# A fused FNet and GEGLU kernel: the first stage in another order

## The chip, the cores and the metric

The kernel runs on one core of a Trainium2 chip. The metric is the device time of one execution in microseconds (us). The engines are named as in the profile: PE is TensorE, PEld its weight loads, DVE is VectorE, ACT is ScalarE, POOL is GpSimd, and SP is SyncE, whose queue issues every DMA.

## What is computed

```python
# x: 2048 rows of 448, fp32; _A_ref is a two-sided DFT (hidden, then sequence; real part)
xn = _layernorm(x)
s = _A_ref(xn, dft_seq_re, dft_seq_im, dft_hid_re, dft_hid_im)
g = silu((gelu(xn @ w_gate) * (xn @ w_up)) @ w_down)      # w_gate, w_up: 448 x 1792
out = x + s * g
```

Every matrix product keeps fp32 accuracy by splitting operands: a rounded part ("high", written by ACT or DVE as fp32r) and the rest ("low", the source minus the high part, written by DVE). A product then is three matmuls: high by high, high by low, low by high.

## The kernel before, in words

The 2048 rows are four chunks (0 to 3) of 512 rows; a chunk is four tiles of 128 rows. The 1792 columns of the feed-forward part are seven groups of two blocks of 128. The order of instructions is written out by hand: the whole body stands under `tc.manual_schedule()`, so each engine executes its own instructions in the order in which the source issues them, and waits at an instruction until what that instruction reads is there. DMAs are issued by SP in the same way, in source order.

The change concerns the first stage, the first 80 us or so, which handles the first group (`GROUPS[0]`) for all four chunks. The steps in it:

- `load_x(c, k0, k1)` (L87) loads tiles of chunk c into `xr`; `load_w(f)` (L167) loads the gate and up weights of one block into one of two `raw` buffers, `load_d` (L219) the down weights of a group, in turn into the same two buffers.
- `stats(c, k0, n)` returns four steps for the layernorm of n tiles. `one(i)` is a BATCH_NORM_STATS (L95) and a BATCH_NORM_AGGREGATE (L96) on DVE for one tile. `root()` is one ACT square root over all n tiles (L100) and two small DVE operations (L101, L102), and so waits for every `one`. `newton()` is four small DVE operations (L106 to L110), the first of which needs the square root. `norm(i)` normalises one tile in place, on DVE (L118) or, if asked, on ACT (L115, L116).
- `turn_mm(c, k)` transposes a normalised tile on PE into a PSUM tile `pt` (L127), of which there are two buffers. `turn_split` empties it: the high part by ACT (L132), a plain copy for later by ACT (L133), the low part by DVE (L134). The third transpose of a chunk can only start when the first `pt` has been emptied by all three.
- `prep_w` splits the weights: high by DVE (L179) or ACT (L177), low by DVE (L182, L184). `prep_d` does so for the down weights (L227 on ACT, L228 on DVE or, for the first group before, on POOL).
- `first` (L417) and `gu_mm` (L239) are the gate and up matmuls. Chunks 0 and 1 are done in halves of 256 columns, `half[0]` from tiles 0 and 1, `half[1]` from tiles 2 and 3 of the chunk.
- `act` starts with a gelu on ACT (L261) and returns three steps, named m, h and l in the source: the product of gelu and up (DVE, L264), its high part (ACT, L265) and its low part (DVE, L266).
- `down` and `down_one` (L286) multiply by the down weights. In the first group ACT copies the results into the accumulator (L293).
- `combine(p)` forms four differences on DVE (L143 to L146) for a Strassen scheme used from the second group on, and returns the step that splits them (L82 on ACT, L83 on DVE).

After the first stage six more groups run through `strassen` (L306, L314 and L286), then the DFT along the hidden axis (L683) and the one along the sequence (L756 to L758).

Of the kernel before, what the change touches and what calls it, by code (L numbers as in the profile page):

```python
# [26 lines left out]
GROUPS = [(f, f + 1) for f in range(0, NF, 2)]  # L27
# [3 lines left out]
def fnet_geglu(ctx: ExitStack, tc: tile.TileContext, x, ct, et, wgu, wd, out):  # L31
# [13 lines left out]
    nc = tc.nc  # L45
# [40 lines left out]
    def load_x(c, k0, k1):  # L86
        nc.sync.dma_start(xr[c][:, k0:k1], xv[:, 4 * c + k0 : 4 * c + k1])  # L87

    def stats(c, k0, n):
        st = const.tile([P, 4, 6], F32, name=f"st{c}_{k0}", tag="st", bufs=2)  # L90
        mv = const.tile([P, 4, 2], F32, name=f"mv{c}_{k0}", tag="mv", bufs=3)
        sd = const.tile([P, 4, 4], F32, name=f"sd{c}_{k0}", tag="sd", bufs=3)

        def one(i):
            nc.vector.bn_stats(st[:, i], xr[c][:, k0 + i, :D])  # L95
            nc.vector.bn_aggr(mv[:, i], st[:, i])  # L96

        def root():
            r, t, w = sd[:, :n, 0], sd[:, :n, 1], sd[:, :n, 2]
            nc.scalar.activation(t, mv[:, :n, 1], AF.Sqrt, bias=epst)  # L100
            nc.vector.tensor_scalar(w, mv[:, :n, 1], EPS, -0.5, op0=ALU.add, op1=ALU.mult)  # L101
            nc.vector.tensor_scalar_mul(sd[:, :n, 3], mv[:, :n, 0], -1.0)  # L102

        def newton():
            r, t, w = sd[:, :n, 0], sd[:, :n, 1], sd[:, :n, 2]
            nc.vector.reciprocal(r, t)  # L106

            nc.vector.tensor_mul(t, r, r)
            nc.vector.tensor_mul(t, t, w)
            nc.vector.scalar_tensor_tensor(r, t, 1.5, r, op0=ALU.add, op1=ALU.mult)  # L110

        def norm(i, eng=nc.vector):
            v = xr[c][:, k0 + i]
            if eng is nc.scalar:
                eng.activation(v, v, AF.Identity, bias=sd[:, i, 3:4])  # L115
                eng.activation(v, v, AF.Copy, scale=sd[:, i, 0:1])  # L116
            else:
                eng.tensor_scalar(  # L118
                    v, v, mv[:, i, 0:1], sd[:, i, 0:1], op0=ALU.subtract, op1=ALU.mult
                )  # L120

        return one, root, newton, norm
# [7 lines left out]
    def turn_split(c, k, pt):  # L130
        sl = slice(k * P, (k + 1) * P)
        nc.scalar.activation(xth[c][:, :, sl], pt, AF.Copy)  # L132
        nc.scalar.activation(xf[c][:, :, sl], pt[:, :2], AF.Copy)  # L133
        nc.vector.tensor_sub(xtl[c][:, :, sl], pt, xth[c][:, :, sl])  # L134
# [26 lines left out]
    def raw_tile():  # L161
        loads[0] += 1
        return a_r[:, 1536 * (loads[0] % 2) :][:, :1536]

    def load_w(f):
        raw = raw_tile()
        nc.sync.dma_start(raw[:, :1024], wgu[f].rearrange("p b f -> p (b f)"))  # L167
        return raw

    def prep_w(slot, raw):  # L170

        w = a_w[:, 2560 * slot : 2560 * slot + 1792]
        wh, wl = w[:, :1024], w[:, 1024:]

        def high(copy):
            if copy is None:
                nc.scalar.activation(wh, raw[:, :1024], AF.Copy)  # L177
            else:
                copy(wh, raw[:, :1024])  # L179

        def low():
            nc.vector.tensor_sub(wl, raw[:, 256:1024], wh[:, 256:])  # L182

            nc.vector.tensor_sub(wh[64:, :256], raw[64:, :256], wh[64:, :256])  # L184

        return high, low, (wh, wl)
# [37 lines left out]
    def prep_d(grp, rv, sub=None):  # L224
        o = 1792 * (grp[0] // 2 % 2)
        w = a_d[:, o : o + 1792].rearrange("p (a f d) -> p a f d", a=2, f=2)
        nc.scalar.activation(w[:, 0], rv, AF.Copy)  # L227
        (sub or nc.vector.tensor_sub)(w[:, 1], rv, w[:, 0])  # L228
        return w

    def gu_mm(ps, w, g, c, cols, late_xtl=False):
        hs, ls = zip(*[block(w, k, g) for k in range(4)])
        hh = [(hs[k], xth[c], k) for k in range(3)]
        hl = [(hs[k], xtl[c], k) for k in range(3)]
        lh = [(ls[k], xth[c], k) for k in range(3)]
        last = [(hs[3], xth[c], 3), (hs[3], xtl[c], 3)]
        mm = hh + lh + last[:1] + hl + last[1:] if late_xtl else hh + hl + lh + last
        for n, (a, xt, k) in enumerate(mm):
            nc.tensor.matmul(ps[:, cols], a, xt[:, k, cols], start=n == 0, stop=n == len(mm) - 1)  # L239
# [8 lines left out]
    def hs_tile(name, dt=FR):  # L248
        return sb.tile([P, 2, 512], dt, name=name, tag="hs", bufs=6)
# [7 lines left out]
    def act(f, c, pg):  # L257
        acts[0] += 1
        gt = tmp(acts[0] % 2)
        hs = new_hs(f, c)  # L260
        nc.scalar.activation(gt, pg[0], AF.Gelu_apprx_tanh)  # L261

        return (
            lambda: nc.vector.tensor_mul(gt, gt, pg[1]),  # L264
            lambda: nc.scalar.activation(hs[:, 0], gt, AF.Copy),  # L265
            lambda: nc.vector.tensor_sub(hs[:, 1], gt, hs[:, 0]),  # L266
        )
# [109 lines left out]
    with tc.manual_schedule():  # L377
        load_x(0, 0, 1)
        load_x(0, 1, 2)
        load_x(0, 2, 4)  # L380
        w_raw = [load_w(0), load_w(1)]
        load_x(1, 0, 4)
        load_x(2, 0, 4)
        load_x(3, 0, 4)
# [39 lines left out]
        one, root, newton, norm = stats(0, 0, 2)  # L424
# [10 lines left out]
        xl = [xtl[0][:, :, k * P : (k + 1) * P] for k in range(4)]  # L435
        nc.scalar.activation(xh[0], t0[2], AF.Copy)
        nc.scalar.activation(xh[1], t1[2], AF.Copy)
        one, root, newton, norm = stats(0, 2, 2)
        one(0)
        one(1)  # L440
        ws = [prep_w(i, w_raw[i]) for i in range(2)]
        ws[0][0](nc.vector.tensor_copy)
        nc.vector.tensor_sub(xl[0], t0[2], xh[0])
        nc.vector.tensor_sub(xl[1], t1[2], xh[1])
        root()
        ws[1][0](None)
        for k, t in enumerate((t0, t1)):
            nc.scalar.activation(xf[0][:, :, k * P : (k + 1) * P], t[2][:, :2], AF.Copy)
        ws[0][1]()
        newton()  # L450
        norm(0)
        norm(1)
# [1 line left out]
        ws = [w[2] for w in ws]  # L454
        draw = load_d(GROUPS[0])
# [4 lines left out]
        one, root, newton, norm = stats(1, 0, 4)  # L460
# [1 line left out]
        one(1)  # L462
        turn_split(*t2)
        turn_split(*t3)
        wdn = prep_d(GROUPS[0], draw, nc.gpsimd.tensor_sub)
        one(2)
        one(3)
        root()
# [8 lines left out]
        turn_split(*t0)  # L477
        turn_split(*t1)
        one, root, newton, norm = stats(2, 0, 4)
        one(0)  # L480
        one(1)
        s_raw = load_w(GROUPS[1][0])
        pg = gu_ps(0, 1)
        gu_mm(pg[0], ws[0], 0, 1, half[0], True)
# [1 line left out]
        gu_mm(pg[1], ws[0], 1, 1, half[0])  # L486
        turn_split(*t2)
        turn_split(*t3)
        m0, h0, l0 = act(0, 0, pgs[0])
        m1, h1, l1 = act(1, 0, pgs[1])  # L490
        m0()
        h0()
        l0()
        gu_mm(pg[0], ws[0], 0, 1, half[1], True)
        gu_mm(pg[1], ws[0], 1, 1, half[1])
        m1()
        h1()
        m0, h0, l0 = act(0, 1, pg)
        one(2)
        l1()  # L500
        one(3)
        root()
        m0()
        h0()
        newton()
        for i in range(4):
            norm(i)
        l0()
        pg = gu_ps(1, 1)
        for g in range(2):  # L510
# [1 line left out]
        one, root, newton, norm = stats(3, 0, 4)  # L512
        one(0)
        one(1)
        xf[2] = hs_tile("xf2", F32)
        turn_split(*turn_mm(2, 0))
        down(0, 0, wdn, [lambda k=k: turn_split(*turn_mm(2, k)) for k in (1, 2, 3)])
        m1, h1, l1 = act(1, 1, pg)
        one(2)
        m1()  # L520
        h1()
        one(3)
        l1()
        root()
        newton()
        norm(0)
        norm(1)

        nws = [None, None]
# [2 lines left out]
        for c in (2, 3):  # L532
            if c == 2:
                draw = load_d(GROUPS[1])
            else:
                s_raw2 = load_w(GROUPS[1][1])
            m0, h0, l0 = gateup(0, c, ws[0])
            between, between1 = [lambda: (m0(), h0()), l0], []
            if c == 2:
                xf[3] = hs_tile("xf3", F32)  # L540
                turn = lambda k: turn_split(*turn_mm(3, k))
                between = [
                    lambda: (m0(), h0(), norm(2)),
                    lambda: (l0(), norm(3), turn(0)),
                    lambda: turn(1),
                    lambda: turn(2),
                ]
                between1 = [lambda: turn(3)]
            down(0, c - 1, wdn, between)
            if c == 2:  # L550
                nws[0] = prep_s(2, s_raw, nc.vector)
            else:
                one = combine(0)
                for i in range(4):
                    one(i)
                nwdn = prep_d(GROUPS[1], draw)
                late_split = combine(1)
            m1, h1, l1 = gateup(1, c, ws[1], between1)
            m1()
            if c == 2:  # L560
                h1()
                l1()
        late = (h1, l1)


# [11 lines left out]
        for gi in range(1, len(GROUPS)):  # L577
            grp = GROUPS[gi]
            nxt = GROUPS[gi + 1] if gi + 1 < len(GROUPS) else None
            ws, wdn = nws, nwdn  # L580
# [226 lines left out]
```

## Time and profile before

| what | value |
|---|---|
| time, median of 3 runs | 813.9 us (813.36 to 814.09) |
| time of the profiled execution | 814.51 us |
| its span, first to last instruction | 812.7 us |
| PE busy | 801.8 us (99%) |
| DVE busy | 415.0 us (51%) |
| ACT busy | 238.7 us (29%) |
| POOL busy | 54.4 us (7%) |
| chain that ended last, PE's share | 95% |
| mean granted PE clock | 0.997 |

The profiled execution is 0.6 us longer than the median, and 1.8 us of its time lie outside its span. Busy shares are averages over the whole span: PE leaves only some 11 us of it idle, so what a change in the order of work is worth has to be read in the windows where PE stands still, by what it waits for there. Times in the trace are counted from the first instruction of the span. A timeline row gives start, duration, engine, line, operation, output and inputs, and in brackets the idle time before it with its releaser.

### The profile page before, as it was taken

What the parts mean: (1) busy time and instruction counts of PE and PEld (TensorE: products, weight loads), DVE (VectorE), ACT (ScalarE), POOL (GpSimd) and SP (SyncE); (2) the same over time, 40 slices, a digit from 0 to 9 for tenths busy, and PEclk for the clock granted to TensorE, in tenths of its full rate; (3) what the DMA queues carried; (4) which work ended last, traced back from release to release, by engine and by line L of the source; (5) the groups of instructions that cost most, each with busy time, mean ns of one, the idle gap of its engine ahead of it and who ended that gap; (6) DMA issues with size and microseconds to landing.
All of it is one profiled execution on the core that took longest, in us unless ns stands there. A gap on an engine that the chain in (4) does not pass through costs nothing.

```text
span 812.7 us, 9386 instructions
## 1 busy us (share of the span) xinstructions
PE 801.8 (99%) x3868; PEld 715.0 (88%) x3868; DVE 415.0 (51%) x626; ACT 238.7 (29%) x356; POOL 54.4 (7%) x62
## 2 busy tenths in 40 slices
PE   8899999999999999999999999999999999999997
PEld 7788888888888888888889999999999999999997
DVE  8776786766776676776763233232232222223221
ACT  3574432322322232232221224122222222222220
POOL 0000120010010010000000000111111111111110
PEclk9999999999999999999999999999999999999999
DMA  8001010000010110100020012344444333444441
GB/s 307 24 0 52 24 52 23 27 27 23 27 49 1 33 43 1 49 23 24 23 77 1 1 38 77 103 140 133 132 127 126 127 127 127 126 127 127 127 127 60
DMA packets 19372, 58.09 MB, mean 71 GB/s; under 512 B 2048, under 2 KB 8064, under 8 KB 18944
## 3 DMA queue, kind: packets, MB, share of 16 engines
q1 hardware_dynamic: 19328, 57.48, 22.1%
q8 instruction: 30, 0.49, 0.2%
q14 instruction: 14, 0.11, 0.0%
HBM read 53.81 MB, written 3.67 MB: 71 GB/s over the span
## 4 chain that ended last, share of the span: by engine, by line
PE 95%; DVE 3%; ACT 1%; issue 1%; DMA 0%; DVEq 0%
PE x L306 22%; PE po L286 16%; PE py L758 13%; PE py L757 13%; PE py L756 13%; PE ab L683 9%; PE x L314 5%; PE gu L239 2%; PE gu L417 1%; PE pt L127 1%; DVE st L95 1%; DVE xr L118 0%; DVE tmp L264 0%; DMA xr<-x 0%; DVE tl L83 0%
## 5 line engine op out<-in xcount | busy, mean ns | idle before, releaser
L286 PE MATMUL po<-wd,hs 128*128 128x448 f32 x672 | 153.0, 366 | 0.0
L286 PEld LDWEIGHTS po<-wd,hs 128*128 128x128 f32 x672 | 125.8, 188 | 14.6 <-ACT gacc L293 0.2
L306 PE MATMUL x<-xt,w 128*128 128x512 f32 x504 | 135.0, 391 | 0.0
L306 PEld LDWEIGHTS x<-xt,w 128*128 128x128 f32 x504 | 94.6, 188 | 17.0
L758 PE MATMUL py<-xt,w 128*128 128x448 f32 x256 | 93.5, 365 | 0.0
L756 PE MATMUL py<-xt,w 128*128 128x448 f32 x256 | 93.5, 365 | 0.0
L757 PE MATMUL py<-xt,w 128*128 128x448 f32 x256 | 93.5, 365 | 0.0
L295 DVE TENSOR_TENSOR gacc<-gacc,po 128x448 f32<-128x448 f32 x96 | 59.3, 618 | 60.8 <-PE po L286 60.8
L306 PE MATMUL x<-th,w 128*128 128x512 f32 x192 | 71.4, 392 | 1.0 <-DVE tmp L264 1.0
L756 PE MATMUL py<-ab,c 128*128 128x448 f32 x192 | 70.1, 365 | 0.0
L757 PE MATMUL py<-ab,c 128*128 128x448 f32 x192 | 70.1, 365 | 0.0
L758 PE MATMUL py<-ab,c 128*128 128x448 f32 x192 | 70.1, 365 | 0.0
L683 PE MATMUL ab<-w,xt 128*128 128x448 f32 x256 | 68.0, 365 | 0.0
L83 DVE TENSOR_TENSOR w<-raw,w 128x1024 fp32r<-128x1024 f32 (+1 forms) x23 | 27.8, 1210 | 73.1 <-ACT w L82 73.1
L82 ACT ACTIVATE w<-raw 128x1024 fp32r<-128x1024 f32 (+1 forms) x23 | 24.2, 1050 | 128.4 <-DMA raw<-ct 118.2
L763 POOL TENSOR_TENSOR gacc<-gacc,s 128x448 f32<-128x448 f32 x15 | 31.0, 2067 | 429.3 <-DVE gacc L762 429.3
L314 PE MATMUL x<-xt,w 128*128 128x512 f32 x192 | 59.2, 389 | 0.0
L762 DVE TENSOR_TENSOR gacc<-gacc,py 128x448 f32<-128x448 f32 (+1 forms) x17 | 10.1, 593 | 87.5 <-PE py L758 87.5
L683 PEld LDWEIGHTS ab<-w,xt 128*128 128x128 f32 x256 | 48.1, 188 | 3.8
L756 PEld LDWEIGHTS py<-xt,w 128*128 128x128 f32 x256 | 48.1, 188 | 3.8
L757 PEld LDWEIGHTS py<-xt,w 128*128 128x128 f32 x256 | 48.1, 188 | 3.8
L758 PEld LDWEIGHTS py<-xt,w 128*128 128x128 f32 x256 | 48.1, 188 | 3.8
(142 smaller groups left out, 1091.1 us busy)
## 6 DMA issues: line engine op xcount, KB each, us to landing
raw<-ct SPq DMA_DIRECT2D x43, 512.0 KB, 4.8
s<-ct SPq DMA_DIRECT2D x21, 512.0 KB, 4.8
raw<-wgu SPq DMA_DIRECT2D x14, 512.0 KB, 3.5
s<-x SPq DMA_DIRECT2D x16, 224.0 KB, 5.2
out<-gacc SPq DMA_DIRECT2D x15, 224.0 KB, 2.0
raw<-wd SPq DMA_DIRECT2D x7, 448.0 KB, 3.3
xr<-x SPq DMA_DIRECT2D x3, 1024.0 KB, 10.9
raw<-et SPq DMA_DIRECT2D x4, 448.0 KB, 3.3
```

The costliest lines, as they stand in the source:

```text
L82: nc.scalar.activation(h, src, AF.Copy)
L83: nc.vector.tensor_sub(l, src, h)
L239: nc.tensor.matmul(ps[:, cols], a, xt[:, k, cols], start=n == 0, stop=n == len(mm) - 1)
L286: nc.tensor.matmul(po[:, :D], hs[:, a, kk * P : (kk + 1) * P], wdn[:, b, i], start=n == 0, stop=n == 5,)
L295: nc.vector.tensor_add(ga, ga, po[:, :D])
L306: nc.tensor.matmul(ps, a[i], b[j], start=first and n == 0, stop=n == 2, skip_group_check=True)
L314: nc.tensor.matmul(ps, w["k3" + "gu"[g]][0], xt[:, 3], start=False, stop=True, skip_group_check=True)
L683: nc.tensor.matmul(p[:, :D], a, b, start=n == 0, stop=n == len(mm) - 1)
L756: nc.tensor.matmul(py[:, :D], a, h, start=k + r == 0, stop=False)
L757: nc.tensor.matmul(py[:, :D], a, l, start=False, stop=False)
L758: nc.tensor.matmul(py[:, :D], b, h, start=False, stop=q == 3 and i == 7)
L763: (nc.vector if last else nc.gpsimd).tensor_add(ga[:, e], ga[:, e], xres[:, e])
```

## The change

It reorders the first stage; no arithmetic is added or left out.

- SP issues the first gate and up weights (`load_w(0)`) as its third DMA, ahead of tiles 2 and 3 of chunk 0, which become the fourth.
- For tiles 2 and 3 of chunk 0, the second `one` and `root` come after the splitting of the first weights instead of before it.
- The low part of the first down weights is formed by DVE instead of POOL, and later: after the l steps of chunk 0, where it had been issued between the second and the third `one` of chunk 1.
- Chunk 2: all four `one` and `root` come before the emptying of chunk 1's third and fourth transposes, where there had been two `one`; `newton` comes before the first gelu, two `norm` between the m, h and l steps of chunk 0, two after `prep_d`. The m and h steps of both blocks now come before their l steps.
- Chunk 3: all four `one` and `root` come before chunk 2's transposes are emptied, where there had been two `one`.
- `combine(0)` is issued after chunk 2 instead of within chunk 3; its splitting stays where it was.
- The order of PE's instructions stays as it was.

```diff
         load_x(0, 0, 1)
         load_x(0, 1, 2)
+        w_raw = [load_w(0)]
         load_x(0, 2, 4)
-        w_raw = [load_w(0), load_w(1)]
+        w_raw.append(load_w(1))
...
+        ws = [prep_w(i, w_raw[i]) for i in range(2)]
+        ws[0][0](nc.vector.tensor_copy)
         one, root, newton, norm = stats(0, 2, 2)
         one(0)
-        one(1)
-        ws = [prep_w(i, w_raw[i]) for i in range(2)]
-        ws[0][0](nc.vector.tensor_copy)
         nc.vector.tensor_sub(xl[0], t0[2], xh[0])
         nc.vector.tensor_sub(xl[1], t1[2], xh[1])
+        ws[1][0](None)
+        ws[0][1]()
+        one(1)
         root()
-        ws[1][0](None)
         for k, t in enumerate((t0, t1)):
             nc.scalar.activation(xf[0][:, :, k * P : (k + 1) * P], t[2][:, :2], AF.Copy)
-        ws[0][1]()
         newton()
...
         turn_split(*t3)
-        wdn = prep_d(GROUPS[0], draw, nc.gpsimd.tensor_sub)
         one(2)
...
         one, root, newton, norm = stats(2, 0, 4)
-        one(0)
-        one(1)
+        for i in range(4):
+            one(i)
+        root()
         s_raw = load_w(GROUPS[1][0])
...
         turn_split(*t2)
         turn_split(*t3)
+        newton()
         m0, h0, l0 = act(0, 0, pgs[0])
         m1, h1, l1 = act(1, 0, pgs[1])
         m0()
         h0()
+        m1()
+        h1()
+        norm(0)
+        norm(1)
         l0()
+        l1()
         gu_mm(pg[0], ws[0], 0, 1, half[1], True)
         gu_mm(pg[1], ws[0], 1, 1, half[1])
-        m1()
-        h1()
+        wdn = prep_d(GROUPS[0], draw)
+        norm(2)
+        norm(3)
         m0, h0, l0 = act(0, 1, pg)
-        one(2)
-        l1()
-        one(3)
-        root()
         m0()
         h0()
-        newton()
-        for i in range(4):
-            norm(i)
         l0()
...
         one, root, newton, norm = stats(3, 0, 4)
         one(0)
         one(1)
+        one(2)
+        one(3)
+        root()
         xf[2] = hs_tile("xf2", F32)
         turn_split(*turn_mm(2, 0))
         down(0, 0, wdn, [lambda k=k: turn_split(*turn_mm(2, k)) for k in (1, 2, 3)])
         m1, h1, l1 = act(1, 1, pg)
-        one(2)
+        newton()
         m1()
         h1()
-        one(3)
+        norm(0)
         l1()
-        root()
-        newton()
-        norm(0)
         norm(1)
...
-                one = combine(0)
                 for i in range(4):
-                    one(i)
+                    late_split(i)
                 nwdn = prep_d(GROUPS[1], draw)
...
             if c == 2:
                 h1()
                 l1()
+                late_split = combine(0)
```

## The prediction

> **What bounds the kernel now.** I read the page first, then the windows of the first 90 us, then the timeline of what ends PE's waits there. The page says that PE is the bound, and that the chain spends only some 5% elsewhere:
>
> ```profile
> PE 801.8 (99%) x3868; PEld 715.0 (88%) x3868; DVE 415.0 (51%) x626; ACT 238.7 (29%) x356; POOL 54.4 (7%) x62
> ...
> PE 95%; DVE 3%; ACT 1%; issue 1%; DMA 0%; DVEq 0%
> ```
>
> So this change is worth what it does to PE's idle time, and to PE's clock. After 18 us PE stands still for 2.10 us at 20.69, 1.15 at 37.88, 0.49 at 42.53 and 1.01 at 80.49. Windows of 1 us, PE alone (busy, then granted clock):
>
> ```profile
> core 0: us, PE busy (x), PEclk, DMA share, GB/s
> 20.00:21.00 1.00, 0.69 (x6) 1.00 0.00 0
> 21.00:22.00 1.00, 0.00 (x0) 1.00 0.00 0
> 22.00:23.00 1.00, 0.21 (x2) 1.00 0.40 77
> 23.00:24.00 1.00, 1.00 (x8) 0.57 0.93 355
> 24.00:25.00 1.00, 1.00 (x6) 0.50 0.07 27
> ...
> 26.00:27.00 1.00, 1.00 (x8) 0.72 0.00 0
> ...
> 37.00:38.00 1.00, 0.88 (x4) 1.00 0.00 0
> 38.00:39.00 1.00, 0.00 (x0) 1.00 0.00 0
> 39.00:40.00 1.00, 0.97 (x7) 1.00 0.00 0
> ```
>
> The wait of 2.10 us is followed by about 3.4 us at half clock (0.57, 0.50, 0.50, 0.72); that of 1.15 us is not. The timeline names the cause of the first and what it costs:
>
> ```profile
> 19.21 2.11 POOL L228 TENSOR_TENSOR wd<-raw,wd 128x896 fp32r<-128x896 f32 x1 [17.91 <-ACT wd L227]
> 19.25 2.10 DVE L101 TENSOR_SCALAR sd<-mv 128x4 f32<-128x4 f32 x1
> ...
> 22.14 1.46 DVE L118 TENSOR_SCALAR xr<-xr,mv,sd 128x512 f32<-128x512 f32 x3
> 22.79 1.61 PE L127 MATMUL pt<-ident,xr 128*128 128x128 f32 x8 [2.10 <-issue]
> 24.05 2.48 PE L417 MATMUL gu<-xt,w 128*128 128x256 f32 x10
> ```
>
> L101 takes 0.17 us elsewhere; beside POOL's subtraction it takes 2.10 and ends with it. The slow clock costs 1.6: eight transposes 1.61 instead of 0.87 (at 14.29), ten L417 matmuls 2.13 in the chain instead of 10 x 0.125. The third and later waits end on DVE:
>
> ```profile
> 40.21 0.69 DVE L266 TENSOR_TENSOR hs<-tmp,hs 128x512 fp32r<-128x512 f32 x1
> 40.81 0.62 DVE L95 BATCH_NORM_STATS2 st<-xr 128x6 f32<-128x448 f32 x1
> ...
> 42.29 1.27 DVE L134 TENSOR_TENSOR xt<-pt,xt 128x512 fp32r<-128x512 f32 x2
> 43.02 0.66 PE L127 MATMUL pt<-ident,xr 128*128 128x128 f32 x4 [0.49 <-DVE xt L134]
> ```
>
> Chunk 2's third transpose waits for L134, which stands behind two `one`. **This is the point to follow**: from 43.02 on PE's work is the same in both kernels and DVE has less left to do, so by how much this transpose comes later or earlier, the end does too.
>
> **Part 1, loads and first weights.** Two DMA answers give the landings:
>
> ```profile
> xr<-x SPq DMA_DIRECT2D x1, 512.0 KB, 4.4
> raw<-wgu SPq DMA_DIRECT2D x1, 512.0 KB, 6.1
> ```
>
> The third DMA (issued 1.63) lands at 6.0, the fourth (2.10) at 8.2. Both are 512 KB, so I let them trade landings: weights at 6.0, rows at 8.2. DVE is free at 6.99 after two L118, as before. L179 takes 0.58 start to start: 7.57. The first `one` now waits for the rows until 8.2 (0.63 lost; none if they land by 7.5, the other bound). Steps from there, start to start: `one` 0.76, two subtractions 0.60 each, L182 0.99, L184 0.45, which gives 11.60. The second `one` ends its aggregate 0.84 later, 12.44; L106 follows 0.37 after that because the square root is no longer hidden behind L182; newton 0.80, two L118 0.92, L182 0.98, L184 0.45: chunk 1's statistics start at 15.96 instead of 14.97, **0.99 late**. PE starts earlier (9.28 becomes about 8.9) but is held by DVE again at the transposes.
>
> **Part 2, POOL's subtraction gone.** L101 comes at 20.24, takes 0.17, and L106 follows at 20.57, 0.33 after L101 started as at 4.95 to 5.28. Three L118 start at 21.37 instead of 22.14, the first transposes at 21.93 instead of 22.79, and at full clock. The second L134 starts at 24.20 (transposes 22.39 to 22.83, ACT's L132, L133, L132, L133 at 0.49 and 0.26 apart from 22.56): chunk 2's statistics start at 24.80 instead of 25.95, **1.15 early**. So removing 2.10 of stall and 1.6 of slow clock leaves 1.15 here.
>
> **Part 3, four `one` and the root of chunk 2 ahead.** Four instead of two: 3 x 0.76 + 0.84 = 3.1, aggregate at 27.93. The wait that this adds is L100's on ACT, and behind it in ACT's queue stand L132 and L133 of chunk 1's last two transposes, for which `half[1]` on PE waits. Before, L132 started at 28.39 by PE's own pace; now at 28.2 by the root, with the second done at 29.55. PE, now faster, is there at 27.70: **a new stall of about 1.85 us**. PE's `half[1]` starts at 29.57 instead of 29.91. The gelu, 2.95 after the first L132 as before (the table load of 1.28 in it), comes at 31.15 instead of 31.34, the first L264 at 31.77.
>
> **Part 4, DVE from there to 43.02.** Start to start: L264 twice 1.2, `norm` twice 0.92, L266 twice 1.2, L228 now on DVE 1.0 (1.08 at 76.98), `norm` twice 0.92, which is 37.0; L264 0.69, ACT's L265 0.63, L266 0.61: 38.98. Four `one` of chunk 3: 42.1. L100 is again ahead of L132 on ACT, so L132 comes at 42.35, L133 at 42.84, L134 at 43.24, and PE's third transpose at **43.95 instead of 43.02: 0.93 late**. PE reaches it at about 40.65 (22 matmuls of 256 columns 2.75, 22 of 512 5.03, two transposes 0.88, twelve L286 2.42): **a new stall of about 3.3 us** in place of 1.15 + 0.49.
>
> **Part 5, edits at nothing.** Two ACT table loads fewer (1.28 each) fall where ACT waits for DVE or PE. The second L219 leaves SP when L228 is done, some 15 us later, and lands well ahead of its L227 at 76.0; behind it in SP's queue is only the L167 that waits until 63.23 in any case. The third L167 moves by 1 us, and its first reader is L200 at 59.60. `combine(0)` goes into DVE's wait of 2.89 before 68.68; yet its split still waits for ACT's L82 at 73.91, behind the last L293, so PE's 1.01 at 80.49 stays. Were the split not held there, the move could gain PE up to that 1.01; were DVE not idle before 68.68, the four subtractions would cost up to 2.8.
>
> **Part 6, the clock, and the sum.** A stall of 2.10 was followed by the slow clock, one of 1.15 was not; 3.3 is beyond both, so I charge 1.6 after it. The stall of 1.85 lies between them, nearer to 2.10. If it too slows PE, that costs nothing itself, since the 3.3 absorbs 1.6 of it. Span: 812.7 + 0.93 + 1.6 = 815.2; with the 1.8 outside, 817.0; the median stands 0.6 below the profiled execution: **816.4 us**.
>
> [...]
>
> **Rivals.** [...] *Rows 2 and 3 land in time*: 0.63 less on the forecast, 815.8. Against: the fourth place landed at 8.2. *The freed stall is kept* (clearly faster): if ACT took L132 ahead of the root, both new stalls would go and 2.10 + 1.6 come off, 810.2; against it stands ACT's strict order in every row here. *Both stalls cost 1.6 in full*: 818.0, only if DVE's chain slips along with PE.
>
> **How the numbers follow.** Forecast 0.50, rows in time with the drop 0.10, both stalls 0.05: slower 0.65. No slow clock 0.31, the same: this kernel's measurement tells about 0.2% (1.6 us) from no change, and 0.93 is less. Faster 0.04. The range runs from 814.2 (no slow clock, rows in time) to 817.6 (the slow clock 1.7, and 1 us for the twenty-odd durations of the chain); the forecast alone is 815.6 to 817.4.
>
> **What would show it.** Right: L101 at about 20.2 with 0.17; L95 of tiles 2 and 3 waiting for a DMA until 8.2; PE idle before `half[1]` near 28 to 29.5, released by ACT L132; PE idle from 40.7 to 43.9, released by DVE L134; clock 0.50 for 3.4 us after it. Wrong: a third transpose of chunk 2 well before 43, or full clock through 50 us.

## The result, and the profile after

The changed kernel takes 816.9 us (median of 8 executions, 816.33 to 818.05), the kernel before, measured beside it, 814.0 (median of 8, 812.90 to 815.95). The ratio is 1.0035 [1.0023, 1.0048]: slower by some 2.9 us. The prediction was 816.4, with a range from 814.2 to 817.6. The profiled execution of the changed kernel took 816.81, its span is 815.0, 2.3 longer than before's 812.7. Two executions of the experiments, of 1740 and 1619 us, lie far outside all others and are left out of every median below.

First the page. PE's work is the same (802.0 busy, x3868); POOL has one instruction less, DVE one more, ACT two less. In the chain, DVE's and a DMA's shares have grown by a point each:

```profile
span 815.0 us, 9383 instructions
...
PE 802.0 (98%) x3868; PEld 714.7 (88%) x3868; DVE 414.6 (51%) x627; ACT 235.7 (29%) x354; POOL 52.0 (6%) x61
...
PE 94%; DVE 4%; ACT 1%; DMA 1%; issue 0%; SPq 0%; DVEq 0%
```

The waits of PE between 12 and 100 us (line that waited, releaser, us in total, times, longest) give the list of places in which to look. The wait of 2.1 at 20.7 is gone; the two longest are new:

```profile
PE pt L127 <- DVE xt L134: 2.9, 1, 2.9
PE gu L239 <- ACT xt L132: 1.6, 1, 1.6
PE x L306 <- DVE tmp L264: 1.0, 1, 1.0
```

The timeline of the changed kernel at those places (start, duration, engine, line, operation; in brackets the idle time before it and what ended it):

```profile
8.62 0.63 DVE L95 BATCH_NORM_STATS2 st<-xr 128x6 f32<-128x448 f32 x1 [0.61 <-DMA xr<-x]
...
16.35 0.63 DVE L95 BATCH_NORM_STATS2 st<-xr 128x6 f32<-128x448 f32 x1
...
20.63 0.17 DVE L101 TENSOR_SCALAR sd<-mv 128x4 f32<-128x4 f32 x1
...
22.43 1.13 PE L127 MATMUL pt<-ident,xr 128*128 128x128 f32 x8 [0.36 <-issue]
...
28.43 0.30 ACT L100 ACTIVATE sd<-mv,epst 128x4 f32<-128x4 f32 x1 [3.69 <-DVE mv L96]
28.63 0.58 ACT L132 ACTIVATE xt<-pt 128x512 fp32r<-128x512 f32 x1
...
30.02 8.07 PE L239 MATMUL gu<-xt,w 128*128 128x256 f32 x44 [1.58 <-ACT xt L132]
...
42.46 0.30 ACT L100 ACTIVATE sd<-mv,epst 128x4 f32<-128x4 f32 x1 [2.39 <-DVE mv L96]
42.67 0.58 ACT L132 ACTIVATE xt<-pt 128x512 fp32r<-128x512 f32 x1
...
43.55 0.69 DVE L134 TENSOR_TENSOR xt<-pt,xt 128x512 fp32r<-128x512 f32 x1 [0.84 <-ACT xf L133]
44.29 1.12 PE L127 MATMUL pt<-ident,xr 128*128 128x128 f32 x4 [2.87 <-DVE xt L134]
```

Read it in pairs. Twice ACT stands idle (3.69 and 2.39) until DVE's aggregate lets L100 go, and only then comes the L132 that stands behind L100 in ACT's queue; twice PE waits for what follows that L132. Without POOL beside it L101 takes 0.17. The windows of PE alone (start and end, length, PE busy and count, granted clock, DMA share, GB/s) show what the second stall brings with it:

```profile
41.00:42.00 1.00, 0.43 (x3) 1.00 0.00 0
42.00:43.00 1.00, 0.00 (x0) 1.00 0.00 0
43.00:44.00 1.00, 0.00 (x0) 0.84 0.00 0
44.00:45.00 1.00, 0.71 (x4) 0.50 0.00 0
45.00:46.00 1.00, 1.00 (x5) 0.50 0.00 0
46.00:47.00 1.00, 1.00 (x4) 0.50 0.00 0
47.00:48.00 1.00, 1.00 (x8) 0.95 0.00 0
```

The clock is at half from 43.68 to 47.10, of which 0.61 still lies in the stall. Further on the chain has the same groups in both kernels (start, duration, engine, output and line). Before:

```profile
44.88 0.44 PE pt L127 x4
...
54.45 1.49 PE po L286 x6
...
61.04 7.53 PE gu L239 x33
```

and in the changed kernel:

```profile
47.46 0.44 PE pt L127 x4
...
57.07 1.23 PE po L286 x6
...
63.36 7.54 PE gu L239 x33
```

The last of them is 2.32 later, which is the difference of the spans. So all of the loss arises ahead of it, in three terms: the third transpose of chunk 2 starts 1.27 later (44.29 for 43.02); from it to the fourth (44.88 and 47.46) PE takes 3.17 for 1.86, 1.31 more, at half clock; and six L286 that took 1.49 before, at 54.45, take 1.23. 1.27 + 1.31 - 0.26 = 2.32.

The first term has to be split once more, as executions do not all get their data at the same time. Chunk 1's statistics begin at 16.35 for 14.97, 1.38 later:

```profile
14.97 0.63 DVE L95 BATCH_NORM_STATS2 st<-xr 128x6 f32<-128x448 f32 x1
```

Counted from there, the third transpose comes after 28.05 before and after 27.94 here. So in this pair of profiles all of the 1.27 is there ahead of chunk 1's statistics; behind them the freed stall and the two new ones cancel, but for 0.11. The experiments say what each of them is worth.

### The profile page after: what moved, and what is told of

Read it like the earlier page. It is cut to its first block, busy times and chain, and to the rows that moved or that the text cites. A ratio compares the mean times of both kernels' runs of the same rounds, so it can differ in the third digit from the quotient of the medians.

```text
span 815.0 us, 9383 instructions
## 1 busy us (share of the span) xinstructions
PE 802.0 (98%) x3868; PEld 714.7 (88%) x3868; DVE 414.6 (51%) x627; ACT 235.7 (29%) x354; POOL 52.0 (6%) x61
## 4 chain that ended last, share of the span: by engine, by line
PE 94%; DVE 4%; ACT 1%; DMA 1%; issue 0%; SPq 0%; DVEq 0%
PE x L306 22%; PE po L286 16%; PE py L759 13%; PE py L757 13%; PE py L758 13%; PE ab L684 9%; PE x L314 5%; PE gu L239 2%; DVE st L95 1%; DMA xr<-x 1%; PE pt L127 0%; PE gu L418 0%; DVE xr L118 0%; DVE tmp L264 0%; ACT xt L132 0%
## 5 line engine op out<-in xcount | busy, mean ns | idle before, releaser
L286 PE MATMUL po<-wd,hs 128*128 128x448 f32 x672 | 153.9, 367 | 0.0
L286 PEld LDWEIGHTS po<-wd,hs 128*128 128x128 f32 x672 | 126.6, 189 | 14.4
```

The lines of the kernel that those rows point to most:

```text
L286: nc.tensor.matmul(po[:, :D], hs[:, a, kk * P : (kk + 1) * P], wdn[:, b, i], start=n == 0, stop=n == 5,)
```

## The experiments

Theory: the loss comes from two orders in ACT's and DVE's queues, the root of chunk 2 ahead of L132 and all of chunk 3's statistics ahead of the emptying, with the slow clock as the second stall's price; what the freed POOL wins is taken back by the first of them. Rivals: the loads and the first weights lose the time; the clock costs nothing; DVE's subtraction is the gain by itself.

Each kernel ran with the kernel before on the same chip; ratios are to that one. First, the changed kernel with one thing altered each time.

**Chunk 3's statistics back where they were, all else changed.**

```diff
         one(1)
-        one(2)
-        one(3)
-        root()
...
         m1, h1, l1 = act(1, 1, pg)
-        newton()
+        one(2)
         m1()
         h1()
-        norm(0)
+        one(3)
         l1()
+        root()
+        newton()
+        norm(0)
         norm(1)
```

> Only chunk 3's statistics go back to their old place: two one ahead of chunk 2's emptied transposes, the other two, root and newton behind. My theory: L134 comes 1.5 (two one) and some 1.1 (the wait for the root on ACT) earlier, the third transpose finds at most 0.3 us of stall, the clock does not fall: 2.6 + 1.3 less, time 812.4 to 813.2, span about 811, under the kernel before. Rival, the late rows of the new load order are the loss: the stage stays late by its 0.6 to 1.0, 816 or more. Rival, the down weights' subtraction on DVE is the loss: it still stands on DVE's chain, 816 or more.

Measured: 813.6 (812.56 to 814.89, 11 executions), ratio 0.9993 [0.9984, 1.0002]; the span is 811.5. The timeline:

```profile
39.16 0.58 ACT L132 ACTIVATE xt<-pt 128x512 fp32r<-128x512 f32 x1
...
41.38 1.27 DVE L134 TENSOR_TENSOR xt<-pt,xt 128x512 fp32r<-128x512 f32 x2
...
42.10 0.66 PE L127 MATMUL pt<-ident,xr 128*128 128x128 f32 x4 [0.20 <-DVE xt L134]
```

L132 comes at 39.16 for 42.67, the wait of 2.87 shrinks to 0.20, and the clock stays at 1.00 behind it. This execution reached chunk 1's statistics at 16.84; counted from there the third transpose comes after 25.26 instead of 27.94, the 2.7 that were expected. 1.0035 to 0.9993 is about 3.4 us: this one order is worth more than the whole loss. The rest of the change, first stall of 1.6 included, is then about even with the kernel before.

**The root of chunk 2 behind the emptying of chunk 1's last two transposes.**

```diff
             one(i)
-        root()
         s_raw = load_w(GROUPS[1][0])
...
         turn_split(*t3)
+        root()
         newton()
```

> Only chunk 2's root is issued behind the emptying of chunk 1's third and fourth transposes instead of ahead of it; its four one stay where they are. My theory: L132 then starts at PE's own pace near 26.7, the first stall falls from 1.58 to about 0.5, and the table load and gelu come 1.0 to 1.5 earlier; the chain on DVE to the third transpose moves with them, while the second stall stays (2.5 to 2.9) and the clock falls after it: time 815.2 to 815.9. Rival, the first stall is hidden by the second and costs nothing: 816.9. Rival, late rows: 816.9.

Measured: 815.5 (814.08 to 816.51, 11), ratio 1.0010 [1.0001, 1.0019], the span 812.9. Timeline of PE:

```profile
30.32 1.94 PE L239 MATMUL gu<-xt,w 128*128 128x256 f32 x14 [0.36 <-DVE xt L134]
...
43.47 0.66 PE L127 MATMUL pt<-ident,xr 128*128 128x128 f32 x4 [2.75 <-DVE xt L134]
```

The first stall falls from 1.58 to 0.36, and the third transpose comes 0.82 earlier (43.47 for 44.29), though this execution reached chunk 1's statistics 0.69 later (17.04 for 16.35). Counted from there it comes after 26.43 instead of 27.94: the 1.22 of the stall and 0.3 more are passed on to the third transpose, and the second stall stays as it was (2.75 for 2.87). And though that stall is 2.75 long, the clock of this execution does not fall behind it:

```profile
43.00:44.00 1.00, 0.53 (x5) 1.00 0.00 0
44.00:45.00 1.00, 1.00 (x8) 1.00 0.00 0
```

What kept it up was not shown; the last section sets this stall beside the others.

**The second stall filled with work.** Eleven matmuls whose result is overwritten stand in PE's queue ahead of the third transpose, so that PE isn't idle there; they write the PSUM tile of the next step ahead of it, and nothing else is altered.

```diff
-        pg = gu_ps(f, c)
+        pg = pg2 if (f, c) == (0, 2) else gu_ps(f, c)
...
+        pg2 = gu_ps(0, 2)
+
+        def fill(n):
+            for _ in range(n):
+                nc.tensor.matmul(pg2[0], ws[0][0][:, :P], xth[1][:, 0], start=True, stop=True)
+
-        down(0, 0, wdn, [lambda k=k: turn_split(*turn_mm(2, k)) for k in (1, 2, 3)])
+        down(0, 0, wdn, [lambda k=k: (fill(11 if k == 2 else 0), turn_split(*turn_mm(2, k))) for k in (1, 2, 3)])
```

> Eleven matmuls of 512 columns, whose result is overwritten later, are put on PE ahead of the third transpose of chunk 2, into the idle 2.87 us of the changed kernel; nothing else is touched. My theory (the second stall delays the stage by 1.27 us and lets the clock fall, which costs 1.3): the transpose stays at 44.3, PE is granted the full clock after it, and the span falls from 815.0 by 1.0 to 1.4, to some 813.8 (time about 815.6). If the clock would have fallen for another reason (the first stall, or the load order), or if the half clock costs nothing in the end: 816.9 as before, give or take 0.3.

Measured: 816.44 (815.07 to 817.97, 11), ratio 1.0027 [1.0018, 1.0036], the span 814.0. Windows and, below, the timeline of this kernel's PE:

```profile
43.00:44.00 1.00, 1.00 (x6) 1.00 0.00 0
44.00:45.00 1.00, 0.63 (x6) 1.00 0.00 0
45.00:46.00 1.00, 1.00 (x8) 1.00 0.00 0
```

```profile
44.57 0.66 PE L127 MATMUL pt<-ident,xr 128*128 128x128 f32 x4 [0.37 <-DVE xt L134]
```

The clock stays at 1.00, and the transpose comes no earlier than with the stall: in this profile the lateness without the idleness does not drop the clock. The other executions agree: of eleven, eight have a mean clock of 0.999 or 1.000, of the changed kernel's thirteen only two. (One period of half clock, 3.41 us of 815, takes 0.002 off the mean; this profile is at 1.00 from 6.51 to 102.09 us, and where its 0.999 arises was not shown.) Within profiles the price is as expected: the second profile of the changed kernel (below) has a span 1.7 longer, of which 0.4 is its later transpose (44.96), so 1.3 is the clock's. The medians differ by only 0.4 to 0.5 (0.5 to 0.7 by the ratios, whose intervals overlap), a miss against the 1.0 or more that was expected. Why is open. In the five executions of the second run of the changed kernel, spans with a mean clock of 1.000 were 814.4 to 814.6, with 0.998 they were 815.0 to 815.7, with 0.996 it was 816.3; but in the first eight the span does not follow the clock (814.8 with 0.995, 814.5 with 0.996, up to 816.3 with 0.998), so something else, such as the landings, moves it by as much.

**Loads and first statistics as before, all else changed.**

```diff
-        w_raw = [load_w(0)]
         load_x(0, 2, 4)
-        w_raw.append(load_w(1))
+        w_raw = [load_w(0), load_w(1)]
...
-        ws = [prep_w(i, w_raw[i]) for i in range(2)]
-        ws[0][0](nc.vector.tensor_copy)
         one, root, newton, norm = stats(0, 2, 2)
         one(0)
+        one(1)
+        ws = [prep_w(i, w_raw[i]) for i in range(2)]
+        ws[0][0](nc.vector.tensor_copy)
...
-        ws[1][0](None)
-        ws[0][1]()
-        one(1)
         root()
+        ws[1][0](None)
...
+        ws[0][1]()
         newton()
```

> The loads and the first statistics, weights and roots stand as in the kernel before; the rest is as in the changed kernel. [...] Rival, the late rows are the loss: 814.0 or less, with no stall of more than 1.2 us.

Measured: 816.1 (815.21 to 817.57, 8), ratio 1.0026 [1.0016, 1.0036]. Chunk 1's statistics start here at

```profile
15.62 0.63 DVE L95 BATCH_NORM_STATS2 st<-xr 128x6 f32<-128x448 f32 x1
```

for 16.35, the third transpose at 43.56 for 44.29: 0.73 earlier in both places, passed on in full. That is less than the loads are worth, as the data land at other times in each execution. In the three kernels measured beside this one that keep the new loads, these statistics start at 16.61, 16.84 and 17.04, that is 1.0 to 1.4 later than here. Over all twelve profiles they start at 14.97 to 16.23 with the old loads and first statistics, and at 16.35 to 17.25 with the new ones, 1.2 later on average. The median is 0.7 to 0.8 lower, though by the intervals of the ratios that alone would not be certain. So the loads are part of the loss, about 1 us, and the rival that they are all of it (814.0 or less, with no stall of more than 1.2) falls. The profile itself shows 815.8, longer than the changed kernel's, because in that execution two periods of half clock stand one behind the other, from 42.81 to 49.64.

**The changed kernel once more**, for its spread and a second profile.

> The changed kernel once more, as the reference on the chip of this call, where the third DMA lands about 1 us later than in the first profile. [...] If the clock never depended on the stalls, every profile would show the drop at the same place.

Measured: 816.82 (816.15 to 818.04, 5), ratio 1.0033 [1.0021, 1.0045]; stalls of 1.58 and 2.9, half clock from 44.40 to 47.81.

Next, the kernel before with only the subtraction of the down weights altered. **On DVE, at its old place:**

```diff
-        wdn = prep_d(GROUPS[0], draw, nc.gpsimd.tensor_sub)
+        wdn = prep_d(GROUPS[0], draw)
```

> The kernel before, with the low part of the first down weights on DVE instead of POOL and nothing else changed, at its old place in the order. My theory: DVE, which executes in order, now waits there for ACT's L227 (18.2 to 19.1, bound by its DMA) with two one behind it, so L106 comes at 22.1 instead of 21.3 and PE's wait grows from 2.1 to 2.9: 0.4 to 0.8 more than the kernel before, 814.7 to 815.1. Rival, the shared stall of POOL and DVE is all that costs there: 1.08 instead of 2.10, about 1 us less, 813.0 to 813.4.

Measured: 815.41 (813.76 to 816.26, 11), ratio 1.0009 [1.0000, 1.0018]. The timeline:

```profile
18.53 0.95 ACT L227 ACTIVATE wd<-raw 128x896 fp32r<-128x896 f32 x1 [1.72 <-DMA raw<-wd]
19.52 1.09 DVE L228 TENSOR_TENSOR wd<-raw,wd 128x896 fp32r<-128x896 f32 x1 [1.37 <-ACT wd L227]
...
22.12 0.17 DVE L101 TENSOR_SCALAR sd<-mv 128x4 f32<-128x4 f32 x1
...
23.93 1.59 PE L127 MATMUL pt<-ident,xr 128*128 128x128 f32 x8 [2.82 <-issue]
```

L101 is short again, but DVE now waits 1.37 for L227, whose weights have just landed, before it can do L228. The stall is 2.82 instead of 2.10, so no POOL beside DVE is not a gain by itself. **On DVE, at the changed kernel's place:**

```diff
-        wdn = prep_d(GROUPS[0], draw, nc.gpsimd.tensor_sub)
         one(2)
...
         gu_mm(pg[1], ws[0], 1, 1, half[1])
+        wdn = prep_d(GROUPS[0], draw)
         m1()
```

> The kernel before, with the low part of the first down weights on DVE and issued where the changed kernel issues it, behind chunk 0's l step; all else as before. My theory: the wait of 2.10 at 20.7 falls to about 0.4 and the clock does not fall there (3.3 us less at that point), DVE has 1.0 more to do before chunk 2's norm, so PE's wait at 37.9 grows from 1.15 to about 2.2, after which the clock may fall: 811.3 without, 812.6 with the fall (in the median of several windows about 812). Rival, DVE's extra microsecond costs as much as POOL's stall: 813.5 to 814.3.

Measured: 813.67 (812.82 to 815.00, 11), ratio 0.9992 [0.9984, 1.0001]; it was to be about 812, so this is half a miss. PE's waits in its timeline, and its windows:

```profile
21.84 1.13 PE L127 MATMUL pt<-ident,xr 128*128 128x128 f32 x8 [0.37 <-issue]
...
38.02 1.06 PE L127 MATMUL pt<-ident,xr 128*128 128x128 f32 x4 [2.40 <-issue]
```

```profile
36.00:37.00 1.00, 0.00 (x0) 1.00 0.00 0
37.00:38.00 1.00, 0.00 (x0) 1.00 0.00 0
38.00:39.00 1.00, 0.98 (x5) 0.53 0.00 0
39.00:40.00 1.00, 1.00 (x5) 0.50 0.08 16
```

The wait of 2.10 at 20.7 is 0.37 here. PE then comes sooner to chunk 2's first transpose and waits 2.40 there for 1.15 before; that transpose starts 1.0 earlier (38.02 for 39.02), though this execution reached chunk 1's statistics 0.79 later (15.76 for 14.97), and in it the slow clock is paid there instead. So in this profile part of the gain went into the next wait on DVE's chain, and the price of the clock moved along with it. Eight of the eleven executions have a mean clock of 1.000, so most do not pay it; why the median did not fall to 812 is open.

Last, kernels that keep the parts that help. **The best of both:** the changed kernel with chunk 3's statistics, the loads and the first statistics as in the three diffs above, and the root of chunk 2 behind the emptying; besides, `combine(1)` is issued later:

```diff
                 nwdn = prep_d(GROUPS[1], draw)
-                late_split = combine(1)
             m1, h1, l1 = gateup(1, c, ws[1], between1)
...
                 late_split = combine(0)
+            else:
+                late_split = combine(1)
         late = (h1, l1)
```

> The changed kernel with what my theory calls its losses undone: loads and first statistics as before, chunk 3's statistics as before, chunk 2's root behind the emptying of chunk 1's transposes; and, for PE's wait of 1.01 near 80, combine(1) issued behind chunk 3's last m step. My theory: no PE wait over 0.6 after 12 us, full clock throughout, 5 to 6 us less than the kernel before: 808.3 to 809.3. Rival, POOL's place or the load order matter more than the roots: not under 811.

Measured: 809.7 (809.12 to 810.53, 5), ratio 0.9942 [0.9930, 0.9955], the span 808.7: faster than both, and the rival (not under 811) falls. All that is left of the three long waits is one of 0.4, in the waits of PE from 8 us on (the first belongs to the start: DVE comes to L179 at 9.62, behind the two `one` whose rows land at 8.1):

```profile
PE gu L417 <- DVE w L179: 1.6, 1, 1.6
PE gu L239 <- DVE xt L134: 0.4, 1, 0.4
```

The full clock throughout that was expected did not come: behind that first wait the clock is at half from 11.58 to 14.99.

**The same with `combine(1)` where the changed kernel has it:**

> As the fastest kernel so far, but combine(1) again where the changed kernel has it, ahead of chunk 3's last m step. My theory: PE's wait of 1.0 near 80 is back and nothing else: 1.0 us more than that kernel, 0.9954 of the kernel before, some 810.7. Rival, the wait near 80 is covered elsewhere: no difference.

Measured: 811.2 (810.29 to 811.57, 6), ratio 0.9965 [0.9953, 0.9977], 0.0023 or some 1.9 us above the best kernel where 1.0 was expected; the intervals overlap, and the trace shows 1.0. The wait that both given kernels have near 80 is back:

```profile
77.00:78.00 1.00, 0.19 (x1) 1.00 0.79 324
```

and with the later `combine(1)`, the same window of the best kernel:

```profile
77.00:78.00 1.00, 1.00 (x7) 1.00 0.88 352
```

In DVE's queue of this kernel the four subtractions of `combine(1)` stand between L228 (73.69) and the L264 (77.47) that PE waits for; in the best kernel that L264 follows L228 (74.18) at 75.76. So the wait is cured by taking these four out of the way, although the split ahead of them still waits for ACT, as the prediction had it.

**The best kernel with the changed kernel's loads and first statistics:** in it the reordered start, loads and first statistics, is the only difference from the best one. Of its diff, the loads:

```diff
         load_x(0, 1, 2)
+        w_raw = [load_w(0)]
         load_x(0, 2, 4)
-        w_raw = [load_w(0), load_w(1)]
+        w_raw.append(load_w(1))
```

> As the fastest kernel so far, but with the loads and first statistics of the changed kernel (first weights as third DMA, rows 2 and 3 as fourth). My theory: the statistics of rows 2 and 3 come 0.6 to 1.0 us later and DVE carries that on to the transposes, against a gain of 0.3 to 1.6 at the first matmuls that PE loses again there: 0.5 to 1.0 more than that kernel, about 810.5. Rival, weights first are the better order once the later stalls are gone: 809.0 or less.

Measured: 810.87 (810.06 to 811.18, 5), ratio 0.9963 [0.9950, 0.9975], 0.0021 or some 1.7 us above the best kernel, with intervals that just overlap; chunk 1's statistics start at 17.25, for 16.23 in the kernel above that was measured beside it. The first weights ahead of rows 2 and 3 lose here too, and the rival (809.0 or less) falls.

## Why the prediction was right

By its steps:

- **Part 1** had the sign and the mechanism, and was a little small. The rows landed at 8.6, not 8.2, and DVE's wait was 0.61 for the 0.63 foreseen. Chunk 1's statistics start 1.38 late in this pair of profiles and 1.2 late over all of them, instead of 0.99.
- **Part 2**: L101 at 20.63 with 0.17, transposes at 22.43, chunk 2's statistics 0.57 early instead of 1.15; the 0.39 of Part 1 explains most of the difference.
- **Part 3**: the stall is 1.58 (foreseen 1.85), `half[1]` at 30.02 (29.57), the gelu at 31.56 (31.15). Both starts are later by some 0.4, what Part 1 missed; that the root ahead of L132 causes it, the second experiment shows.
- **Part 4**, the step that decides: the third transpose at 44.29 instead of 43.95, so 1.27 late and not 0.93; the difference is Part 1's. Counted from chunk 1's statistics, the sum had 0.06 of gain (0.99 less 0.93) and the traces show 0.11, so the balance of the freed stall against the two new ones was right. From the gelu on, the sum of DVE's steps was right within 0.1. The stall is 2.87 for 3.3, as PE too arrived later.
- **Part 5**: the table loads cost nothing visible, and the wait near 80 stayed at 1.0. Its cause was named too narrowly: without the four subtractions behind the split there is no wait, though the split is as late.
- **Part 6**: the clock cost 1.31 in the profile for 1.6, because 0.61 of the period of 3.41 still lay within the stall, which costs nothing. The 0.26 that went near 54.45 were not in the sum. The three errors, +0.34, -0.29 and -0.26, leave 2.32 for the 2.53 that was summed up.

Two figures agree by more luck than this shows. The sum for one execution was near (817.0, measured 816.81), but the forecast then took off the 0.6 by which the profiled execution of the kernel before stands above its median. The changed kernel's stands at its median (816.81 for 816.9), so nothing was to be taken off, and the forecast of 816.4 came out 0.5 low. And the second stall's clock, 1.31 in the profile, is by the filled stall worth only 0.4 to 0.7 between medians. The kernel before pays for the clock in some executions, too: near 812 of span at a mean clock of 1.000, near 813.5 at 0.997. How much of the 2.9 between the medians is the clock of either kernel was not separated.

"No slow clock", with its chance of 0.31, holds for two of the changed kernel's thirteen executions, by their mean clock of 1.000. What kept the clock up in them was not shown, as neither is profiled; in the profile with the stall of 2.75 it stayed at 1.00, too. Of the rivals, "the freed stall is kept" named the right remedy for one stall only. With L132 ahead of the root of chunk 2 alone the ratio is still 1.0010; chunk 3's L132 has to come ahead of two `one` and the root, too.

## What to carry to other kernels

ACT, with its queue in strict order, served PE here only as early as the instruction ahead of it let it: with statistics that end in one square root over four tiles put ahead of the copies that empty PSUM, ACT stood idle for 3.69 and 2.39 us until the fourth tile was done, and PE for 1.58 and 2.87. So after an edit that frees a stall, follow the shared engine on to the next place where PE meets it, and compare the start of the first instruction from which PE's work is the same; here a stall of 2.10 less, and its slow clock, came out together with the two new stalls as 0.11 earlier. Count in both kernels from a common point behind the loads: with one and the same order of loads, chunk 1's statistics started anywhere from 14.97 to 16.23, a spread wider than most of the terms in question. And look at granted clock and mean clock of several executions before a term of the clock goes into a sum about medians.

## What the runs showed of the hardware

**Half clock came in periods of 3.41 us, behind some of PE's stalls.** Within the first 100 us of the profiles each period of half clock is 3.41 us long (23.14 to 26.56 in the kernel before, 43.68 to 47.10 in the changed kernel), or twice that (42.81 to 49.64 in the kernel with the loads as before). PE's stalls, its idle time in the 3.41 us ahead of the fall of the clock, and the clock behind the stall:

| Kernel | stall, us | idle in the 3.41 us ahead of the fall, us | clock after it |
|---|---|---|---|
| before, at 37.9 | 1.15 | no fall | full |
| after, first stall | 1.58 | no fall | full |
| root of chunk 2 behind, second stall | 2.75 | no fall | full |
| best, `combine(1)` as in after, at 10 us | 1.62 and 0.2 | no fall | full |
| best, at 10 us | 1.59 and 0.16 | 1.74 | half |
| before, at 20.7 | 2.10 | 2.10 | half |
| loads as before, second stall | 2.88 | 2.13 | half |
| after, second stall | 2.87 | 2.25 | half |
| subtraction on DVE, late | 2.40 | 2.40 | half |
| subtraction on DVE, old place | 2.82 | 2.82 | half |

The length of the stall alone does not tell the two apart: behind 2.10 to 2.9 the clock was at half in six profiles (the five here and the second one of the changed kernel) and at full in one, with 2.75, and with some 1.6 and 0.2 near 10 us it was at half in one profile and at full in another. What else decides was not shown. Nor was what keeps a clock at half: in the kernel with the loads as before, a period of half clock in which PE idled for 0.75 was followed by a second one, while in the changed kernel one with 0.61 was not.

**A small DVE instruction beside POOL's large one ended with it.** The 128x4 L101 took 2.10, from 19.25 to 21.35, beside the 128x896 subtraction, from 19.21 to 21.32, in the one profile that has them side by side; at the same place it took 0.17 in the changed kernel (20.63) and with the subtraction on DVE (22.12 and 20.03).
